# Mirrored rows of x from a reversed copy in DRAM, in a Fourier mixing layer with a gated feed-forward layer

## The chip, the cores and the metric

The kernel runs on one core of one Trainium2 chip. The metric is device time in microseconds; the time before is a median of 654.22 us over three runs (650.11 to 654.27). The engines are named as in the profile: PE does matmuls, PEld loads their weights, DVE, ACT and POOL are the vector, scalar and GpSimd engines, and SP issues most of the DMAs.

## The reference

```python
# x: (8, 3008, 256)
X = np.fft.fft(x, axis=1)
X = np.fft.fft(X, axis=2)
t = X.real.astype(np.float32).reshape(24064, 256)
gate = np.maximum(t @ w_gate, 0.0)          # w_gate, w_val: 256 x 1536
val = t @ w_val
out = (gate * val @ w_out).astype(np.float32)  # w_out: 1536 x 256
```

## The kernel before, in words

Only the real part of the two transforms is wanted, so each batch of 3008 rows is first *folded*: rows are added to and subtracted from their mirror images along the sequence and along the channels. What is left is a set of small cosine and sine matmuls (`family`, `dft_steps`), whose results `U` and `V` feed the feed-forward layer. The transform over the channels is multiplied into the weights beforehand (`WA`, `WB`, `WM`). Channel 128 goes a way of its own: `channel_128` writes it to `FN`, a set of "Nyquist" matmuls at L445 reads `FN`, and its row goes through DRAM (`ch128`) and comes back, spread over all partitions, as `CB` (L780) and as one row of `V` (L783).

**Folding.** A batch comes into `XD` by plain DMAs in natural order (`load_rows`, L94 and L98: six DMAs of about 256 KB and two of one row each) and into `XG` in mirrored order (`load_mirror`, L102: six indirect DMAs that POOL issues, each with a list of row numbers). Two rows of x lie side by side in a "pair" of 512 numbers; the half `r` of a batch has 752 pairs, of which 376 are wanted in reverse. `fold_steps(b)` is a list of (cost, step): six `fold_a` (L113), a small one, `channel_128` (L147, L148), then `load_rows(b + 1)`, six `fold_pq` (L121), `small` (L159, L161), and last `fold_f` and `fold_g` (L128, L137) twice each, with the six gathers of batch b + 1 between them. All of this is POOL's work, except that batch 0 is folded on DVE and POOL.

**When fold steps run.** A batch from 1 on has 36 slots (`slot`), three blocks of twelve, each slot for one tile of 128 hidden channels by 504 (or 497) columns in two mirrored halves. In a slot, PE runs five matmuls of 504 columns and eight output matmuls (L498) of the block before; ACT seeds a bank (L686) and copies (L694); DVE combines (L702) and multiplies (L599); POOL adds (`both`, L703). `run_fold` then adds a credit and takes steps from the list while the credit pays for them; at the end of a batch `run_fold(99)` takes all that are left. The credit is 1.1 x 0.9 in batch 1 and 0.9 x 0.9 in later ones. In batch b, `fold_steps(b + 2)` runs. Batch 0 is done in four segments instead; there POOL folds batches 1 and 2 without slots, up to the last six entries of batch 2, which go over into batch 1.

**Outputs.** A finished output tile is copied by ACT into `os` (L504), which has four buffers, and goes out by two or three DMAs on SP (L513, L516). SP works through its DMAs in program order: outputs, `load_rows`, `ch128`, `CB`, `V`. The build gives each DMA one of eight completion counters in turn, so an issue also waits for the DMA eight issues earlier.

The places that set this order:

```python
    for k in range(6):
        steps += gathers[k:k + 1] + last[k:k + 1]
...
    run_fold(fold_us * (1.6 if not new else .9))
    run_one(evict)
```

Of the kernel before, what the change touches and what calls it, by code (L numbers as in the profile page):

```python
# [10 lines left out]
F32 = mybir.dt.float32  # L11
# [21 lines left out]
def kernel(  # L33
# [8 lines left out]
    nc = tc.nc  # L42
# [57 lines left out]
    def load_mirror(b, t, r):  # L100
# [3 lines left out]
            in_offset=bass.IndirectOffsetOnAxis(ap=gidx[0:n, 2 * t + r:2 * t + r + 1] if t < 2 else gidx2[0:n, r:r + 1], axis=0),  # L104
            element_offset=b * S * D)

    def flat(ap):
        return ap.rearrange("p t q d -> p (t q) d")

# [29 lines left out]
    def fold_steps(b):  # L139

        e, p, ts = nc.gpsimd, slice(0, 128), slice(0, 3)
        steps = [(1.1, lambda r=r, t=t: fold_a(e, p, r, t)) for t in range(3) for r in range(2)]
        steps += [(0.2, lambda: e.tensor_tensor(XG[:, :, :, ::-1, 0], XG[:, :, :, ::-1, 0], XD[:, :, :, :, 0], op=ALU.add))]

        def channel_128():
            for i in range(2):
                e.tensor_tensor(c128p[:, i], XG[:, 0, :, ::-1, 128], XG[:, 1, :, ::-1, 128], op=SIGN[i])  # L147
            e.tensor_tensor(FN[:, :, :, :, b // 2, :, b % 2].rearrange("p i t q h -> p i (t q) h"),  # L148
                            c128p[:].rearrange("p i t q -> p i (t q)").unsqueeze(3).to_broadcast([128, 2, 6, 2]), sg[:], op=ALU.mult)
        steps.append((0.5, channel_128))  # L150
        gathers = []
        if b + 1 < B:
            steps.append((0.0, lambda: load_rows(b + 1)))
            gathers = [(1.3, lambda r=r, t=t: load_mirror(b + 1, t, r)) for t in range(3) for r in range(2)]
        steps += [(1.1, lambda i=i, t=t: fold_pq(e, p, i, t)) for t in range(3) for i in range(2)]

        def small():
            for i in range(2):
                e.tensor_tensor(PQ[:, i, :, :, 0], XG[:, 0, :, ::-1, 0], XG[:, 1, :, ::-1, 0], op=SIGN[i])  # L159
            zero = PQ[:, :, :, :, 0:1].rearrange("p i t q d -> p (i t q) d")  # L160
            e.tensor_tensor(FF[b % 2][:, :, :, :, 0:1].rearrange("p i t q d -> p (i t q) d"), zero, zero, op=ALU.add)  # L161
        steps.append((0.6, small))
        last = []
        for fam in (1, 0):
            last.append((1.7, lambda fam=fam: fold_f(e, p, ts, fam, b)))
            last.append((1.7, lambda fam=fam: fold_g(e, p, ts, fam, b)))
        for k in range(6):
            steps += gathers[k:k + 1] + last[k:k + 1]
        return steps

    load_rows(0, nc.scalar)

# [175 lines left out]
    for n, c in enumerate(order):  # L348
        even_rest(n, c)
        load_mirror(1, n // 2, n % 2)  # L350

# [351 lines left out]
    def slot(cur, mid, nxt, after, outs, fold_us):  # L705

        stop = len(todo_out)

        def out(part):
            run(todo_out, len(todo_out) - stop + outs * part // 8)  # L710
        old = nxt is not None and nxt["kind"] == "o"
        new = nxt is not None and not old
        if old:
            gate(nxt)
        if new and mid["kind"] != "o":
            sine_part(nxt)
        out(3)
        out(5)
        if new and mid["kind"] == "o":
            sine_part(nxt)  # L720
        if new:
            cosine_part(nxt)
        seed(after)
        if pending is not None:
            mirror(pending["v"], pending, 1)
        if pending is not None:
            second(pending)
        value(cur)
        if cur["kind"] == "o":
            mult(cur, 0, cur["first"])  # L730
        else:
            relu_mult(cur, 0)
        if new:
            both(nxt)
        if old:
            nxt["first"] = nxt["r"]
            mirror(nxt["g"], nxt, 0)
            relu(nxt)
        run_fold(fold_us * (1.6 if not new else .9))
        run_one(evict)  # L740
        run_one(sums)
        out(8)
        return cur
# [4 lines left out]
    for b in range(B):  # L748
        blocks = thirds if b else segments
        more_b = {} if b else more  # L750
        if 0 < b < B - 2:
            todo_fold += fold_steps(b + 2)
        for blk, block in enumerate(blocks):
            hs = []
            if (b, blk) == (0, 1):
                todo_dft = dft_steps(0, U, V, (0,), nyq=True, now=True)
            if b == 0 and blk > 1:
                todo_fold = fold_steps(blk - 1)
                later = todo_fold[-6:] if blk == 3 else []
                del todo_fold[len(todo_fold) - len(later):]  # L760
                run_fold(99)
                todo_fold = later
            if blk == (0 if b else 2) and b + 1 < B:
                Un, Vn = new_uv()
                todo_dft = dft_steps(b + 1, Un, Vn, (1, 0), now=not b)
                CBn = up.tile([128, 4 * NJ + 2], BF16, name="CB", tag="CB")
                uv[b + 1] = Un, Vn, CBn
                steps, todo_dft = todo_dft, []
                if b == 0 or b % 2:
                    g, N = (b + 1) // 2, rp.tile([36, NE], BF16, name="N", tag="N", bufs=1)  # L770
                    todo_dft = nyquist_steps(g, N)

                    def keep(N=N, g=g):
                        flush()
                        keep_nyquist(g, N)
                    first = 0 if b == 0 else 18
                    steps[first] = lambda step=steps[first], keep=keep: (keep(), step())

                def row_128(b=b, CBn=CBn):
                    nc.sync.dma_start(out=CBn[:, 0:4 * NJ + 1], in_=dram(ch128, (b + 1) * (4 * NJ + 1), [[0, 128], [1, 4 * NJ + 1]]))  # L780

                def row_0(b=b, Vn=Vn):
                    nc.sync.dma_start(out=Vn[0:1, 0:4 * NJ + 1], in_=ch128[b + 1:b + 2, :])  # L783
                for at, f in ((6 if b == 0 else 21, row_128), (21, row_0)):
                    steps[at] = lambda step=steps[at], f=f: (f(), step())
                todo_dft = todo_dft + steps if b == 0 else steps[:18] + todo_dft + steps[18:]
            per_tile = len(todo_out) // NF
            paired = b > 0
            if (b, blk) == (0, 0):
                for fi in range(NF):  # L790
                    st = tile_of(block, fi, (U, V, CB))
                    add_h(st, hs)
                    pending = first_tile(st, more.get((0, fi), ()))
                mirror(pending["g"], pending, 0)
                relu(pending)
            elif not paired:
                for fi in range(NF):
                    st = tile_of(block, fi, (U, V, CB))
                    add_h(st, hs)
                    tag = {(3, 8): "g", (3, 9): "d", (3, 10): "g", (3, 11): "d"}.get((blk, fi), "p")  # L800
                    last = []
                    if (blk, fi) == (3, 11):
                        last = [lambda: (sine_part(ahead[1]), cosine_part(ahead[1]), both(ahead[1]), seed(ahead[2]))]
                    if (blk, fi) == (3, 9):
                        ahead = [next(tiles) for _ in range(3)]
                        more[(3, 9)] = [lambda: seed(ahead[0], prime())]
                        more[(3, 10)] = [lambda: seed(ahead[1], prime())]
                        more[(3, 11)] = [lambda: (sine_part(ahead[0]), cosine_part(ahead[0]), both(ahead[0]))]
                    pending = single_tile(st, per_tile // 2, more_b.get((blk, fi), ()), last, tag)
                    run(todo_dft, DFT_0[blk - 1][fi])  # L810
            else:
                for fi in range(NF):
                    at = NF * blk + fi
                    cur = ahead.pop(0)
                    add_h(cur, hs)
                    ahead.append(next(tiles, None))
                    pending = slot(cur, *ahead, per_tile, 1.1 if b == 1 else .9)
                    run(todo_dft, DFT_ODD[at] if b % 2 else DFT_EVEN[at])
            run(todo_out, len(todo_out))
            if blk == len(blocks) - 1 or (b, blk) == (0, 1):  # L820
                run(todo_dft, len(todo_dft))
            todo_out = out_steps(b, block, hs)
        if b:
            run_fold(99)
        if b + 1 < B:
            U, V, CB = Un, Vn, CBn
# [31 lines left out]
```

## Time and profile before

| | |
|---|---|
| median of three runs | 654.22 us |
| profiled execution: its time, its span | 654.64 us, 652.4 us |
| mean granted clock of PE | 0.992 |
| busy PE, DVE, POOL, ACT | 95%, 85%, 83%, 70% of the span |
| DMA, mean | 85 GB/s |
| the chain that ended last | PE 67%, DVE 13%, POOL 9% |
| `both` (L703) | 252 x 1251 ns |
| `fold_a` (L113), `fold_pq` (L121) | 42 x 1260 ns, 42 x 1089 ns |
| gathers (L102) | 48 x 1016 ns, 3.7 us to landing |

Busy shares are means over stages with different limits: the first 30 us are tables and weights, batch 0 lasts to about 112 us, and then come seven batches of some 65 to 75 us. The chain's shares tell which engine's work stood last before what followed it, not what would be won if that work were shorter. The granted clock is the share of its full rate that PE's clock was let run at.

### The profile page before, as it was taken

What the parts mean: (1) busy time and instruction counts of PE and PEld (TensorE: products, weight loads), DVE (VectorE), ACT (ScalarE), POOL (GpSimd) and SP (SyncE); (2) the same over time, 40 slices, a digit from 0 to 9 for tenths busy, and PEclk for the clock granted to TensorE, in tenths of its full rate; (3) what the DMA queues carried; (4) which work ended last, traced back from release to release, by engine and by line L of the source; (5) the groups of instructions that cost most, each with busy time, mean ns of one, the idle gap of its engine ahead of it and who ended that gap; (6) DMA issues with size and microseconds to landing.
All of it is one profiled execution on the core that took longest, in us unless ns stands there. A gap on an engine that the chain in (4) does not pass through costs nothing.

```text
span 652.4 us, 12167 instructions
## 1 busy us (share of the span) xinstructions
PE 621.8 (95%) x4140; PEld 401.4 (62%) x4142; DVE 553.1 (85%) x988; ACT 455.3 (70%) x822; POOL 542.0 (83%) x516
## 2 busy tenths in 40 slices
PE   0999999997998999999999999999999999999996
PEld 0356676564665666666666666666666666666665
DVE  8875566995996889989899889989899989999991
ACT  8697666774775777777777777777777777777751
POOL 8589995898999999999899999999986666666660
PEclk9999999997998999999999999999999999999999
DMA  8922653223222422214222332221211121111112
GB/s 224 205 66 63 193 147 99 63 65 128 83 71 78 141 74 80 76 52 143 89 82 79 104 96 92 68 65 40 65 49 33 47 70 52 33 48 49 49 47 80
DMA packets 42438, 55.24 MB, mean 85 GB/s; under 512 B 5153, under 2 KB 32353, under 8 KB 42376
## 3 DMA queue, kind: packets, MB, share of 16 engines
q1 hardware_dynamic: 34552, 39.23, 19.7%
q0 software_dynamic: 7536, 14.72, 8.9%
q8 instruction: 32, 0.52, 0.3%
q10 hardware_dynamic: 288, 0.52, 0.2%
q14 instruction: 30, 0.25, 0.1%
HBM read 32.14 MB, written 24.67 MB: 87 GB/s over the span
## 4 chain that ended last, share of the span: by engine, by line
PE 67%; DVE 13%; POOL 9%; issue 7%; ACT 3%; DMA 0%; DVEq 0%; SPq 0%; ACTq 0%; POOLq 0%
PE o L498 27%; PE v L577 7%; DVE h L599 7%; PE v L572 6%; PE v L573 6%; PE g L691 6%; PE p L698 5%; POOL r L703 5%; DVE r L702 5%; PE d L387 3%; POOL XG L102 1%; PE p L577 1%; POOL XG L113 1%; PE p L573 1%; PE p L572 1%
## 5 line engine op out<-in xcount | busy, mean ns | idle before, releaser
L703 POOL TENSOR_TENSOR r<-r 128x504 f32<-128x504 f32 (+1 forms) x252 | 313.2, 1251 | 73.7 <-DVE r L702 72.6
L599 DVE SCALAR_TENSOR_TENSOR h<-r,v 128x504 bf16<-128x504 f32 (+1 forms) x504 | 318.6, 673 | 51.4 <-PE v L577 34.4
L498 PE MATMUL o<-wo,h 128*128 128x256 bf16 x2304 | 347.0, 273 | 0.0
L498 PEld LDWEIGHTS <-h 128*128 128x128 bf16 x2304 | 226.0, 98 | 116.7 <-issue 3.9
L686 ACT ACTIVATE p<-CB,b 128x504 f32<-128x504 bf16 (+1 forms) x252 | 172.4, 684 | 74.1 <-DVE r L702 72.3
L694 ACT COPY r<-g 128x504 f32<-128x504 f32 (+1 forms) x252 | 145.6, 578 | 76.6 <-PE g L691 72.0
L702 DVE SCALAR_TENSOR_TENSOR r<-r,p 128x504 f32<-128x504 f32 (+1 forms) x252 | 168.8, 670 | 0.6 <-ACT r L694 0.6
L577 PE MATMUL v<-V,WM 128*128 128x504 bf16 (+3 forms) x296 | 109.1, 368 | 3.7 <-DVE h L599 3.1
L572 PE MATMUL v<-U,WA 128*128 128x504 bf16 (+3 forms) x296 | 109.1, 369 | 0.1
L573 PE MATMUL v<-V,WB 128*128 128x504 bf16 (+3 forms) x296 | 109.0, 368 | 0.0
L691 PE MATMUL g<-V,WM 128*128 128x504 bf16 (+1 forms) x252 | 95.2, 378 | 0.4 <-ACT r L694 0.3
L698 PE MATMUL p<-U,WA 128*128 128x504 bf16 (+1 forms) x252 | 95.0, 377 | 0.0
L595 DVE TENSOR_TENSOR h<-r,v 128x376 bf16<-128x376 f32 (+1 forms) x88 | 44.7, 543 | 25.6 <-PE v L577 13.6
L504 ACT COPY os<-o 128x512 f32<-128x512 f32 x96 | 55.6, 579 | 14.1 <-PE o L498 7.1
L572 PEld LDWEIGHTS <-WA 128*128 128x128 bf16 x348 | 34.0, 98 | 42.4 <-issue 13.1
L102 POOL DMA_INDIRECT XG<-in_x_dram,gidx x48 | 48.8, 1016 | 8.8 <-issue 6.8
L573 PEld LDWEIGHTS <-WB 128*128 128x128 bf16 x348 | 34.1, 98 | 35.2 <-issue 1.2
L113 POOL TENSOR_TENSOR XG<-XG,XD 128x510 f32<-128x510 f32 x42 | 52.5, 1260 | 0.1
L587 ACT ACTIVATE r<-p 128x376 f32<-128x376 f32 (+1 forms) x80 | 38.3, 490 | 18.6 <-PE p L577 11.4
L121 POOL TENSOR_TENSOR PQ<-XG 128x510 f32<-128x510 f32 x42 | 45.3, 1089 | 0.0
L577 PEld LDWEIGHTS <-WM 128*128 128x128 bf16 x348 | 34.1, 98 | 7.7 <-issue 0.2
L691 PEld LDWEIGHTS <-WM 128*128 128x128 bf16 x252 | 24.8, 98 | 6.8 <-issue 1.3
(130 smaller groups left out, 380.0 us busy)
## 6 DMA issues: line engine op xcount, KB each, us to landing
out_dram<-os SPq DMA_DIRECT2D x118, 128.0 KB
XD<-in_x_dram SPq DMA_DIRECT2D x30, 256.0 KB
out_dram<-os SPq DMA_DIRECT2D x62, 120.0 KB
XD<-in_x_dram SPq DMA_DIRECT2D x16, 240.0 KB
CB<-ch SPq DMA_DIRECT2D x7, 376.2 KB
out_dram<-os SPq DMA_DIRECT2D x10, 127.0 KB
XG<-in_x_dram,gidx POOLq DMA_INDIRECT x48, 3.7
h<-in_moe_w_gate_dram POOLq DMA_DIRECT2D x3, 256.0 KB, 7.0
```

Of the source, the lines that this page charges most:

```text
L113: e.tensor_tensor(XG[p, r, t, ::-1, 1:D], XG[p, r, t, ::-1, 1:D], XD[p, r, t, :, D - 1:0:-1], op=ALU.add)
L498: nc.tensor.matmul(st["p"][:, q, :], lhsT=hs[f][:, sign, h0:h0 + 128], rhs=wo[:, f, :], start=(f == 0), stop=(f == NF - 1))
L572: nc.tensor.matmul(bank[:, 0:st["n"]], lhsT=WA[i][:, st["f"]], rhs=st["us"], start=True, stop=False)
L573: nc.tensor.matmul(bank[:, 0:st["n"]], lhsT=WB[i][:, st["f"]], rhs=st["vs"], start=False, stop=True)
L577: nc.tensor.matmul(bank[:, 0:st["n"]], lhsT=WM[i][:, st["f"]], rhs=st["vs"], start=False, stop=True, skip_group_check=True)
L599: nc.vector.scalar_tensor_tensor(half_h(st, sign), in0=st["s"][1 + sign][:, 0:n], scalar=0.0, in1=st["v"][:, 0:n], op0=ALU.max, op1=ALU.mult)
L686: nc.scalar.activation(st["p"][:, 0:st["n"]], st["c"], ACTF.Copy, scale=b2[:, st["fi"]:st["fi"] + 1])
L691: nc.tensor.matmul(st["g"][:, 0:n], lhsT=WM[0][:, st["f"]], rhs=st["vs"], start=True, stop=True)
L694: nc.scalar.copy(q[:, 0:n], st["g"][:, 0:n])
L698: nc.tensor.matmul(st["p"][:, 0:n], lhsT=WA[0][:, st["f"]], rhs=st["us"], start=False, stop=True, skip_group_check=True)
L702: nc.vector.scalar_tensor_tensor(sp[:, 0:n], in0=q[:, 0:n], scalar=-0.5, in1=st["p"][:, 0:n], op0=ALU.mult, op1=ALU.add)
L703: nc.gpsimd.tensor_tensor(sm[:, 0:n], sp[:, 0:n], q[:, 0:n], op=ALU.add)
```

## The change

For batches 2 to 7, `XG` no longer comes by gathers. `reverse(b)`, one DMA on SP's queue, copies the wanted rows of batch b to a DRAM tensor `xr` in reverse order: its source runs over 2 halves, 376 pairs at a step backward, and 512 numbers; its destination is contiguous. `load_reversed(b)` then brings them to `XG` by six plain DMAs, and one pair of each half by two DMAs of one row. In the list of fold steps, `load_reversed(b + 1)` stands at no cost between the first and the second pair of `fold_f` and `fold_g`, and `reverse(b + 2)` at no cost at the end. `reverse(2)` is issued at the start. Batches 0 and 1 keep the gathers. The credit becomes 1.05 in batch 1 and 0.7 later, without the factor, and four entries of batch 2's list go over into batch 1.

```diff
+    xr = nc.dram_tensor("xr", (B, 2, H // 4, 2 * D), F32).ap()
+
+    def reverse(b):
+
+        n = H // 4
+        nc.sync.dma_start(out=xr[b], in_=dram(x, b * S * D + (H // 2 - 1) * 2 * D, [[H * D, 2], [-2 * D, n], [1, 2 * D]]))
+
+    def load_reversed(b):
+        n = H // 4
+        for t in range(3):
+            m = (128, 128, 120)[t]
+            for r in range(2):
+                nc.sync.dma_start(out=XG[0:m, r, t, :, :].rearrange("p a d -> p (a d)"), in_=xr[b, 1 - r, 128 * t:128 * t + m, :])
+        for r in range(2):
+            nc.sync.dma_start(out=XG[120:121, r, 2, :, :].rearrange("p a d -> p (a d)"),
+                              in_=dram(x, b * S * D + r * H * D, [[0, 1], [1, 2 * D]]))
...
-        gathers = []
         if b + 1 < B:
             steps.append((0.0, lambda: load_rows(b + 1)))
-            gathers = [(1.3, lambda r=r, t=t: load_mirror(b + 1, t, r)) for t in range(3) for r in range(2)]
...
-        for k in range(6):
-            steps += gathers[k:k + 1] + last[k:k + 1]
-        return steps
+        if b + 1 < B:
+            last.insert(2, (0.0, lambda: load_reversed(b + 1)))
+        if b + 2 < B:
+            last.append((0.0, lambda: reverse(b + 2)))
+        return steps + last
...
         load_mirror(1, n // 2, n % 2)
+    reverse(2)
...
-        run_fold(fold_us * (1.6 if not new else .9))
+        run_fold(fold_us)
...
-                later = todo_fold[-6:] if blk == 3 else []
+                later = todo_fold[-4:] if blk == 3 else []
...
-                    pending = slot(cur, *ahead, per_tile, 1.1 if b == 1 else .9)
+                    pending = slot(cur, *ahead, per_tile, 1.05 if b == 1 else .7)
```

## The prediction

> **What bounds the kernel now.** I read, in this order: the page's busy shares, the windows by batch, the waits, the timelines of PE, POOL and ACT around the two places where PE idles, and last the DMA view.
>
> ```profile
> PE 621.8 (95%) x4140; PEld 401.4 (62%) x4142; DVE 553.1 (85%) x988; ACT 455.3 (70%) x822; POOL 542.0 (83%) x516
> ...
> L102 POOL DMA_INDIRECT XG<-in_x_dram,gidx x48 | 48.8, 1016 | 8.8 <-issue 6.8
> ```
>
> ```profile
> 154.00:161.00 7.00, 6.13 (x27) 2.73 (x28) 1.44 (x3) 2.02 (x4) 5.22 (x8) 0.51 0.88 293
> 205.00:209.00 4.00, 4.00 (x17) 2.17 (x16) 2.96 (x7) 2.47 (x4) 4.00 (x4) 0.57 0.21 64
> ...
> 206.80:281.90 75.10, 75.10 (x498) 48.83 (x497) 67.98 (x117) 53.55 (x93) 73.09 (x67) 0.99 0.29 88
> 281.90:356.90 75.00, 74.94 (x506) 48.47 (x504) 67.75 (x117) 54.13 (x95) 72.04 (x67) 1.00 0.29 89
> 356.90:430.50 73.60, 73.60 (x494) 48.10 (x492) 67.76 (x117) 53.17 (x93) 71.67 (x66) 1.00 0.30 90
> 430.50:505.30 74.80, 74.80 (x506) 48.45 (x504) 67.81 (x117) 54.25 (x95) 64.94 (x59) 1.00 0.16 48
> 505.30:576.00 70.70, 70.70 (x475) 46.25 (x473) 65.83 (x113) 51.20 (x89) 43.79 (x35) 1.00 0.16 50
> ```
>
> The columns after the span are PE, PEld, DVE, ACT, POOL, granted clock, DMA share, GB/s. From batch 2 on PE never idles, and a matmul costs the same with gathers (73.6 us / 494 = 149 ns), without them (74.8 / 506 = 148) and without any fold (70.7 / 475 = 149). POOL's load is therefore hidden there. It shows at two places in batch 1:
>
> ```profile
> PE d L445 <- POOL FN L148: 3.3, 1, 3.3
> PE v L577 <- DVE h L599: 3.1, 4, 2.1
> ...
> 199.57 1.04 POOL L102 DMA_INDIRECT XG<-in_x_dram,gidx  x1 [0.19 <-issue]
> 200.92 1.03 POOL L102 DMA_INDIRECT XG<-in_x_dram,gidx  x1 [0.31 <-issue]
> 203.27 1.27 DVE L599 SCALAR_TENSOR_TENSOR h<-r,v 128x504 bf16<-128x504 f32 x2 [3.00 <-POOL r L703]
> 204.59 0.37 PE L577 MATMUL v<-V,WM 128*128 128x504 bf16 x1 [2.14 <-DVE h L599]
> ```
>
> At 151.6 the Nyquist matmuls wait 3.3 us for `channel_128`, and the clock then stands at half (0.51 over 7 us: 3.4 us lost). At 202.5 two gathers stand ahead of a `both`; PE loses 2.1 us and then 1.7 us to the clock (0.57 over 4 us).
>
> **What is removed.** 36 gathers leave POOL, 36 x 1.016 = 37 us plus some 7 us of issue gaps. The worth is what PE gets: 3.3 + 3.4 + 2.1 + 1.7 = 10.5 us. Batch 1 to its `channel_128` held four gathers (119.7 to 135.8) at about 1.2 us; without them, and at a credit of 1.05 a slot where 1.1 x 0.9 = 0.99 stood, `FN` is ready some 10 us before PE asks, so I take the whole gain. Batches 2 to 4: between 0 and 1 us each (their 148 to 151 ns a matmul against 148 without gathers); I take 1.5 in all. The credits: a `both` (1.25) and 1.05 of fold make 2.3 us of POOL a slot against PE's two; lag costs nothing until `both` is some 3 us late (the 3.00 wait above). Batch 1 may pass that: 0 to 3.5 us, taken as 1. At 0.7 the sum is 1.95 and hidden. Net: **-11 us** (bounds -13.5 and -7).
>
> **What is added on SP.** Per batch, eight loads into `XG` and one copy. The loads are like XD's, some 0.45 us an issue; six XD loads land within 7 us, one slot of 36 needs them, and POOL reads them ten or more slots later. Only in batch 0, where POOL goes straight from fold 1 to fold 2, can POOL wait for them, by some 5 us, before it has a `both` to deliver at 112.7: zero. SP has idle time for 9 issues (it waits 406 us for `os`). They wait for POOL's `small`; the outputs behind them need ACT's `os` later than that: zero too.
>
> The copy `reverse` is another matter. It moves 752 rows of 2 KB, and its source has 2 as its outermost count. How wide does a DMA run? The trace has two of small shape. The output of 127 rows issued at 273.1 ran alone like this (columns: 40 slices of 277.7 to 279.4 us):
>
> ```profile
> GB/s 410 24 313 217 506 24 313 410 313 120 169 506 121 169 24 410 24 72 120 72 24 24 24 24 24 24 24 24 24 24 24 24 24 24 24 24 24 24 24 24
> ```
>
> The peaks are a gather; the floor of 24 GB/s is that output, one row after another, 1 KB in 42 ns: a single engine. `ch<-N` at 317, with 2 outermost on one side and 4 on the other, posts one early completion event and then two: two engines. So I count two engines for `reverse`: 1.54 MB / (2 x 24 GB/s) = **32 us**. Bounds: 30 (25.6 GB/s an engine, a 410 slice above over 16) and 40 (376 rows x 106 ns, the mean of XD's 2 KB packets, which share engines). DRAM to DRAM stands nowhere in the trace; I stay at the low end because nothing else is queued ahead.
>
> And what stands behind it? The 128-row output issued right after that 127-row one got 15 of its 16 completions by 277.2 us and the last at 282.8, when the 127 rows were through. So a DMA on SP's queue waits, on each engine that it shares, for what was issued before. Everything that SP issues within 32 us of a `reverse` lands after it: 1.3 us to start (XD: issue 152.99, first packet 154.3), 32 of copy, 0.7 to land: **34 us** from its issue.
>
> The Trainium skill, page DMA: Bandwidth & Descriptors, section Rules for kernel authors, says that an outermost dimension below 16 confines a DMA to that many engines; here that is 2, as counted. The same page's table in section Bandwidth gives 341 GB/s for 1 MB, by which the copy would take about 4.5 us (an estimate from that table) and the sum would be 642 rather than 682; its rows are for 128 partitions, and the 24 GB/s row above speaks for the first.
>
> **Where that stalls.** `os` has four buffers, so a copy L504 waits until the outputs four tiles back have landed. ACT's copies in steady state:
>
> ```profile
> 254.84 0.58 ACT L504 COPY os<-o 128x512 f32<-128x512 f32 x1
> 260.61 0.58 ACT L504 COPY os<-o 128x512 f32<-128x512 f32 x1
> 266.39 0.58 ACT L504 COPY os<-o 128x512 f32<-128x512 f32 x1
> 272.17 0.58 ACT L504 COPY os<-o 128x512 f32<-128x512 f32 x1
> 280.89 0.58 ACT L504 COPY os<-o 128x512 f32<-128x512 f32 x1
> 284.94 0.58 ACT L504 COPY os<-o 128x512 f32<-128x512 f32 x1
> ```
>
> Behind a stuck L504 ACT holds the next slot's L694 and L686; PE runs on for about one slot, 1.8 us, which I subtract each time.
>
> - `reverse(2)`, about 31 to 65 us: `os` is written first at 49.3, the fifth time at 80. Zero.
> - `reverse(3)`, issued at about 75.5 (after XD's and XG's loads), landed 109.5. In the built program SP waits at the eighth DMA behind it for the copy itself; ten issues later (4.6 us) follows CB's load, behind XD's 1.5 MB (7.7 us from issue to last packet when batch 3's came at 91.6). CB lands at about 118.5; the first L686 wants it at 107.7. 10.8 - 1.8 = 9.
> - `reverse(4)`, about 117.5, landed 151.5; the output behind it has 127 rows on one engine, 5.4 us more: 157. L504 at 151.7 wants that buffer, and the next one is 1 us worse: 6.3 - 1.8 = 4.5.
> - `reverse(5)`, right behind CB's issue at 167.7, landed 201.7, wanted by the copy at 194.6: 7.1 - 1.8 = 5.3.
> - `reverse(6)`, `reverse(7)`: behind the outputs of the copy like 254.84, so issued at 256.2, landed 290.2, wanted at 284.94: 5.3 - 1.8 = 3.5 each.
>
> Together 9 + 4.5 + 5.3 + 3.5 + 3.5 = **25.8 us**. PE idle of 2.1 and 3.3 us was followed by 1.7 and 3.4 us lost to the clock: 2.5 for each of five, **12.7**.
>
> **Sum.** The profiled execution took 654.64 (span 652.4), 0.4 above the median of 654.22: 654.6 - 11 + 25.8 + 12.7 = **682 us**. With 30 us of copy, 1.7 of clock each and 1.2 us more slack, the five stalls shrink by 2.5 each: 654.6 - 13 + 13.3 + 8.5 = 663. With 40 us and 3.4: 654.6 - 9 + 25.8 + 41 + 17 = 729.
>
> **Rivals.**
> 1. The copy does not hold the queue: it spreads over 16 engines or yields to what is behind. For it: 1.5 MB of XD landed in 7 us. Against: the 127-row output and the late sixteenth completion. Then only POOL's relief is left: 654.6 - 11 to - 13.5 = 641 to 643.6, faster. It decides once the copy takes under some 20 us, as then no buffer and no CB is late.
> 2. The stalls of `os` are absorbed (copy of about 27 us, or more slack than a slot), and only CB in batch 0 is late: 654.6 - 11 + 9 + 3.4 = 656, no change. Against: the low bound of the copy is 30.
> 3. DRAM to DRAM rows cost 106 ns or more: 715 to 729. For it: XD's mean under load; against: two engines alone have no neighbour.
> 4. POOL at 2.3 us a slot becomes batch 1's bound: 3.5 instead of 1. It shifts the sum by 2.5 only, to 684.5, and is inside the forecast's range.
>
> **How the numbers follow.** Forecast (with 4) 0.62, its own range 663 to 715; rival 3 0.14; rival 2 0.09; rival 1 0.15. One per cent, 6.5 us, is about what a measurement of this kernel can tell from no change. Faster by more: rival 1, 0.15. Within: rival 2 less its edges, 0.08. Slower: 0.77. The range is 646 to 718: it leaves out most of rival 1 and the upper end of rival 3, under 2 in 10.
>
> **What would show it.** Right: six bursts of about 48 GB/s for 32 us; CB's landing and the first L686 late by about 10 us; L504 waiting for DMA `out_dram<-os` some 5 us, four times; granted clock 0.5 right behind; no wait of L445 for FN. Wrong: copies of 5 us at 300 GB/s, or L504 with no DMA wait, with a span near 640.

## The result, and the profile after

The changed kernel takes a median of 696.3 us (692.97 to 697.5, four runs) beside 652.17 us of the kernel before on the same chip (650.11 to 654.27, four runs): a ratio of 1.067, interval 1.061 to 1.073. It is slower by 44 us. The forecast was 682, in a range of 646 to 718. The profiled execution took 696.21 us, with a span of 694.4 and a mean granted clock of 0.970; the spans differ by 694.4 - 652.4 = 42.0 us. Undisturbed runs of before lie between 650.0 us, with a granted clock of 1.0, and 655.1 us, with 0.992; its profiled execution (654.64 us, 0.992) is one of the longer ones, and only these have lost clock to win back. Line numbers move by 18 in the changed kernel: the copy into `os` is L522, its stores L531 and L534, ACT's seed L704, `CB` L798; `reverse` is L112 and the loads from `xr` L119.

The busy shares of the page, after:

```profile
PE 630.4 (91%) x4142; PEld 403.9 (58%) x4142; DVE 554.2 (80%) x988; ACT 454.2 (65%) x822; POOL 506.7 (73%) x480
```

POOL lost its 36 gathers (542.0 to 506.7 us), as planned, and the end did not come earlier. The windows by batch, after (a window from the first combine of DVE in batches 1 to 5 to that of the next; columns after the span: PE, PEld, DVE, ACT, POOL, granted clock, DMA share, GB/s):

```profile
125.80:206.20 80.40, 75.29 (x479) 46.53 (x478) 66.81 (x114) 53.76 (x95) 69.47 (x61) 0.97 0.35 112
206.20:298.80 92.60, 76.11 (x495) 48.99 (x493) 68.12 (x118) 53.12 (x93) 66.18 (x60) 0.91 0.29 94
298.80:379.50 80.70, 76.70 (x506) 48.92 (x505) 67.85 (x117) 53.77 (x95) 66.16 (x60) 0.98 0.32 102
379.50:459.90 80.40, 76.40 (x495) 49.06 (x493) 68.05 (x118) 53.00 (x93) 66.28 (x60) 0.96 0.32 102
459.90:534.60 74.70, 74.70 (x505) 48.36 (x504) 67.71 (x117) 54.09 (x95) 66.08 (x60) 1.00 0.16 48
```

Batches 2 to 4 took 77.6, 75.0 and 73.6 us before. Now PE idles in each of the first four, and its busy time grows as well, since the clock drops. From batch 5 on, when no copy is issued any more, the old length is back. The stalls themselves, in the timeline of ACT (idle time before the instruction and what ended it in brackets):

```profile
111.40 0.58 ACT L522 COPY os<-o 128x512 f32<-128x512 f32 x1 [6.62 <-DMA out_dram<-os]
121.05 0.69 ACT L704 ACTIVATE p<-CB,b 128x504 f32<-128x504 bf16 x1 [6.35 <-DMA CB<-ch]
172.84 0.58 ACT L522 COPY os<-o 128x512 f32<-128x512 f32 x1 [5.83 <-DMA out_dram<-os]
227.36 0.58 ACT L522 COPY os<-o 128x512 f32<-128x512 f32 x1 [17.80 <-DMA out_dram<-os]
319.96 0.59 ACT L522 COPY os<-o 128x512 f32<-128x512 f32 x1 [5.12 <-DMA out_dram<-os]
400.79 0.58 ACT L522 COPY os<-o 128x512 f32<-128x512 f32 x1 [5.17 <-DMA out_dram<-os]
```

One stall for each copy from `reverse(3)` on, and two for that one. What they make of PE, in the waits:

```profile
PE g L709 <- ACT r L712: 28.4, 4, 16.5
PE g L595 <- ACT r L605: 10.8, 3, 6.5
```

No row names the Nyquist matmuls waiting for `FN` any more. The copies themselves, in the DMA view of 195 to 217 us, while `reverse(5)` runs (40 slices):

```profile
GB/s 59 17 45 67 52 45 52 52 52 52 52 52 52 45 52 52 52 52 52 52 52 45 52 52 52 52 82 52 52 45 52 52 52 52 52 52 52 45 52 52
```

52 GB/s, flat: two engines at 26 GB/s each. The copy's 752 packets of 2 KB lie between 195.2 and 226.2 us: 31 us for 1.54 MB, where the prediction had 48 GB/s and 32 us. And SP's own timeline shows something that the prediction did not have:

```profile
137.74 20.96 SPq L531 DMA_DIRECT2D out_dram<-os  x1
158.74 8.42 SPq L534 DMA_DIRECT2D out_dram<-os  x1
...
168.69 6.95 SPq L94 DMA_DIRECT2D XD<-in_x_dram  x6
...
192.68 0.65 SPq L112 DMA_DIRECT2D xr<-in_x_dram  x1
193.44 24.70 SPq L531 DMA_DIRECT2D out_dram<-os  x1
```

The first store behind a copy, from `reverse(3)` on, holds SP in its issue for 19 to 25 us; before, no issue on SP took over 2.9. The sign was there to read: the three issues of before over 2 us, at 195.5, 273.1 and 421.7 us (2.2, 2.6 and 2.9), each stand right behind a store of 127 rows. One of these stores, issued at 272.8 us, is the one that the prediction read as running on a single engine (it says 273.1). So SP itself is late after a copy, and with it all that stands later in its order.

### The profile page after: what moved, and what is told of

Its sections match the earlier page's. It is cut to its first block, busy times and chain, and to the rows that moved or that the text cites. A ratio compares the mean times of both kernels' runs of the same rounds, so it can differ in the third digit from the quotient of the medians.

```text
span 694.4 us, 12187 instructions
## 1 busy us (share of the span) xinstructions
PE 630.4 (91%) x4142; PEld 403.9 (58%) x4142; DVE 554.2 (80%) x988; ACT 454.2 (65%) x822; POOL 506.7 (73%) x480
## 4 chain that ended last, share of the span: by engine, by line
PE 57%; DVE 16%; DMA 12%; issue 7%; SPq 4%; ACT 4%; POOL 1%; DVEq 0%; ACTq 0%; POOLq 0%
PE o L516 22%; DVE h L617 9%; DVE r L720 6%; PE v L595 6%; PE g L709 5%; PE v L590 5%; PE v L591 5%; PE p L716 5%; DMA out_dram<-os 5%; DMA xr<-in_x_dram 5%; PE d L405 3%; SPq L531 2%; SPq L534 1%; DMA XD<-in_x_dram 1%; DMA CB<-ch 1%
## 5 line engine op out<-in xcount | busy, mean ns | idle before, releaser
L704 ACT ACTIVATE p<-CB,b 128x504 f32<-128x504 bf16 (+1 forms) x252 | 172.6, 685 | 78.0 <-DVE r L720 70.9
L720 DVE SCALAR_TENSOR_TENSOR r<-r,p 128x504 f32<-128x504 f32 (+1 forms) x252 | 169.0, 671 | 27.4 <-ACT r L712 27.4
L522 ACT COPY os<-o 128x512 f32<-128x512 f32 x96 | 55.6, 579 | 56.4 <-DMA out_dram<-os 44.8
L590 PEld LDWEIGHTS <-WA 128*128 128x128 bf16 x348 | 34.2, 98 | 41.7 <-issue 12.7
L145 POOL TENSOR_TENSOR F<-PQ 128x768 bf16<-128x768 f32 (+2 forms) x16 | 27.3, 1708 | 0.0
```

The costliest lines, as they stand in the source:

```text
L522: nc.scalar.copy(os_[:], st["p"][:])
L590: nc.tensor.matmul(bank[:, 0:st["n"]], lhsT=WA[i][:, st["f"]], rhs=st["us"], start=True, stop=False)
L704: nc.scalar.activation(st["p"][:, 0:st["n"]], st["c"], ACTF.Copy, scale=b2[:, st["fi"]:st["fi"] + 1])
L720: nc.vector.scalar_tensor_tensor(sp[:, 0:n], in0=q[:, 0:n], scalar=-0.5, in1=st["p"][:, 0:n], op0=ALU.mult, op1=ALU.add)
```

## The experiments

Stage lengths are read in each kernel's trace from DVE's combines: a batch begins with every 36th. The first column is the time at which batch 1 begins, the next are lengths in us; batch 6 lasts 73.6 us everywhere. The runs of before that were taken beside these kernels have medians of 652.09 to 653.16 us; each ratio is to the runs taken beside that kernel. Batches 1 and 2 of before, with 79.5 and 77.6 us, are longer than the 65 to 75 us said ahead.

| kernel | median us | ratio to before (interval) | batch 1 begins | 1 | 2 | 3 | 4 | 5 |
|---|---|---|---|---|---|---|---|---|
| before | 652.17 | 1 | 111.9 | 79.5 | 77.6 | 75.0 | 73.6 | 74.8 |
| changed | 696.3 | 1.067 (1.061 to 1.073) | 125.8 | 80.5 | 92.5 | 80.8 | 80.3 | 74.8 |
| one early copy | 646.38 | 0.992 (0.990 to 0.995) | 111.7 | 75.8 | 73.6 | 75.0 | 73.6 | 74.8 |
| seven `os` | 660.89 | 1.015 (1.011 to 1.018) | 125.7 | 75.7 | 74.3 | 75.0 | 73.6 | 74.8 |
| pieces | 686.65 | 1.054 (1.051 to 1.058) | 126.1 | 100.3 | 73.9 | 75.0 | 73.6 | 74.8 |
| ACT's queue | 681.46 | 1.047 (1.043 to 1.050) | 130.4 | 91.8 | 73.6 | 75.0 | 73.6 | 74.8 |
| sixteen engines | 646.05 | 0.989 (0.987 to 0.991) | 112.3 | 75.8 | 73.6 | 75.0 | 73.6 | 74.8 |
| 2, 3, 4 joined | 670.96 | 1.027 (1.024 to 1.029) | 112.3 | 75.7 | 86.5 | 81.0 | 80.8 | 74.8 |
| copies alone | 705.01 | 1.078 (1.075 to 1.081) | 125.1 | 87.1 | 85.5 | 86.6 | 84.2 | 74.8 |
| GpSimd's queue | 672.42 | 1.031 (1.028 to 1.035) | 132.0 | 81.0 | 74.6 | 75.5 | 73.5 | 74.8 |
| credits alone | 654.84 | 1.004 (1.002 to 1.006) | 112.0 | 77.5 | 74.6 | 76.7 | 75.2 | 76.5 |
| one early copy, old credits | 645.8 | 0.989 (0.986 to 0.991) | 111.7 | 75.0 | 73.6 | 75.0 | 73.6 | 74.8 |
| the same, seven `os` | 645.58 | 0.990 (0.988 to 0.993) | 111.6 | 75.0 | 73.6 | 75.0 | 73.6 | 74.8 |

**One early copy.** All six batches go as one DMA where `reverse(2)` stood; nothing else is copied later.

```diff
-        nc.sync.dma_start(out=xr[b], in_=dram(x, ..., [[H * D, 2], [-2 * D, n], [1, 2 * D]]))
+        nc.sync.dma_start(out=xr[b:B].rearrange("b h n d -> (b h) n d"),
+                          in_=dram(x, ..., [[H * D, 2 * (B - b)], [-2 * D, n], [1, 2 * D]]))
...
-        if b + 2 < B:
-            last.append((0.0, lambda: reverse(b + 2)))
...
```

The list of fold steps is one entry shorter by this, and three entries of batch 2's list go over into batch 1 in place of four, so the same steps go over. In the other kernels whose list changes by a copy's entry the number is set the same way.

> One copy for batches 2 to 7 where reverse(2) stood (12 halves outermost, so 12 engines), and the five later copies left out; all else as in the changed kernel. Theory: a copy keeps two engines for 31 us and SP, which issues everything else, stands still meanwhile; this is the whole loss. Then the one copy runs from 31 to some 62 us, where no output needs its buffer: no L522 waits for a DMA, CB is on time, and the time is that of before less the 10.5 us that batch 1 lost to POOL: 640 to 644. Rival: the loads into XG, the bytes or the credits carry part of the loss: 655 or more, with the copies out of the way.

Measured 646.38 us, 2 above the expected interval, and 0.8% under the kernel before. All the loss is gone, so the later copies made it, not the loads from `xr` or the credits. Its stages against those of before also give the gain by itself: 3.7 us in batch 1, 4.0 in batch 2, nothing later, 652.4 - 644.6 = 7.8 us of span. Between the medians (652.09 for the runs of before beside it) it is 5.7, because the profiled execution of before, at 654.64 us, lies above that median.

**Seven buffers of `os`.**

```diff
-                os_ = rp.tile([128, 2, D], F32, name="os", tag="os", bufs=4)
+                os_ = rp.tile([128, 2, D], F32, name="os", tag="os", bufs=7)
```

> Seven os buffers where four stood; all else as in the changed kernel. SP is held as before, but ACT has 18 us more before it needs a buffer. Theory (the os buffers carry the loss of reverse(4) to reverse(7), CB's landing that of reverse(3)): waits of L522 under 5 us in all, the first L704 still waits for CB, some 13 us now that no L522 waits ahead of it: 655 to 663. Rival (late XD, XG or CB loads carry the loss in later batches as well): 675 or more.

Measured 660.89 us, inside. Its waits:

```profile
ACT p L704 <- DMA CB<-ch: 13.0, 1, 13.0
...
ACT os L522 <- DMA out_dram<-os: 1.4, 1, 1.4
```

The copies still hold SP's queue (SP stands 25.2 us in the store behind `reverse(5)`), but ACT does not want a buffer before they are through. From batch 1 on the stages are those of one early copy, but for 0.7 us in batch 2. Only `CB`, which no buffer helps, is late, and that is nearly all of the 14.4 us of span left: batch 1 begins at 125.7 us, 14.0 late.

**Sixteen engines.** The same six DMAs, places and bytes, with 16 outermost. This kernel leaves out the mirrored order of the rows, so its results for batches 2 to 7 are not the reference's; it is there for its time alone.

```diff
-        nc.sync.dma_start(out=xr[b], in_=dram(x, ..., [[H * D, 2], [-2 * D, n], [1, 2 * D]]))
+        nc.sync.dma_start(out=xr[b].rearrange("h n d -> (h n) d").rearrange("(a j) d -> a j d", a=16),
+                          in_=dram(x, b * S * D, [[2 * D, 16], [32 * D, n // 8], [1, 2 * D]]))
```

> The six copies of the changed kernel at their places, each with the same 752 rows of 2 KB in SP's queue, but laid out with 16 as the outermost count instead of 2; the rows are taken in another order than the mirrored one, so the values of batches 2 to 7 are not the reference's. Theory (what costs is that a copy sits on two of the sixteen engines for 30.5 us, with SP and the stores of os behind it): at 26 GB/s an engine 1.54 MB are 4 us, with 47 rows on each engine, and the kernel is the one with a single early copy, 645 to 650 us, with no wait for os over 1 us that the kernel with one early copy (2.0 us) does not have, and CB not late. Rival (the bytes, or six more DMAs in SP's row ahead of the outputs, cost, whatever their width): 675 us or more.

Measured 646.05 us, with the waits of one early copy: `os` 2.0 us once, and no row for `CB`.

```profile
ACT os L523 <- DMA out_dram<-os: 2.0, 1, 2.0
```

So neither the bytes nor the place in SP's order cost anything: the width does. The source is also stepped through forward here, but that is not the reason: the one early copy steps backward on twelve engines, and its DMA view has a mean of 307 GB/s between 60 and 61.2 us, 26 GB/s an engine as on two. SP's timeline at `reverse(5)`:

```profile
166.99 0.62 SPq L112 DMA_DIRECT2D xr<-in_x_dram  x1
167.71 13.44 SPq L532 DMA_DIRECT2D out_dram<-os  x6
```

The second row covers six stores and SP's waits for ACT between them; the first store was issued in 0.57 us, not 24.7. The Trainium skill, page DMA: Bandwidth & Descriptors, section Rules for kernel authors, has the rule on which the prediction leaned, that an outermost count under 16 confines a DMA to that many engines at most; the 52 GB/s above and this run agree.

**The copies alone.** The kernel before, gathers and credits included, with the six copies at their places. Nothing reads `xr`.

> The kernel before with its gathers and its credits, and the six copies of the changed kernel added at the changed kernel's places; nothing reads what they write. Theory (the copies alone cost what the change costs and gives back; the reads of the mirrored rows add little): 652.1 + 42 + 7.8 = 695 to 705 us, with the waits for os and for CB of the changed kernel. Rival (the loss needs the new loads of XG in SP's row behind each copy): 655 to 675 us.

Measured 705.01 us, at the upper edge. The copies make the loss with or without the new loads, and the gathers' leaving takes some of it back. The timeline of ACT in this kernel has the same stalls at other lengths, since the order on SP is another; two of them:

```profile
251.76 0.58 ACT L514 COPY os<-o 128x512 f32<-128x512 f32 x1 [6.96 <-DMA out_dram<-os]
336.92 0.59 ACT L514 COPY os<-o 128x512 f32<-128x512 f32 x1 [10.54 <-DMA out_dram<-os]
```

**Copies 2, 3 and 4 joined.** One DMA, outermost count 6, at the place of `reverse(2)`; `reverse(5)` to `reverse(7)` stay.

```diff
+        c = 3 if b == 2 else 1
-        nc.sync.dma_start(out=xr[b], in_=dram(x, ..., [[H * D, 2], [-2 * D, n], [1, 2 * D]]))
+        nc.sync.dma_start(out=xr[b:b + c].rearrange("b h n d -> (b h) n d"),
+                          in_=dram(x, ..., [[H * D, 2 * c], [-2 * D, n], [1, 2 * D]]))
...
-        if b + 2 < B:
+        if 5 <= b + 2 < B:
...
```

> The copies for batches 2, 3 and 4 go as one DMA (outermost count 6) where the copy for batch 2 stands; those for batches 5, 6 and 7 stay. Four buffers of os. Theory (the copy for batch 5 cost 14.9 us in the changed kernel because SP was late from the copy for batch 4 and issued it after the first store of the block, not ahead of it): now it is issued in time and costs what the copies for batches 6 and 7 cost there (5.8 and 6.7); three of them on the kernel with one early copy: 646.4 + 6 to 8 + 5.8 + 6.7 = 665 to 668 us. Rival (the copy for batch 5 has a costly place of its own): 646.4 + 18.7 + 5.8 + 6.7 = 675 to 679 us.

Measured 670.96 us: between the two. The timelines of SP and of ACT, and the window of batch 2, in this kernel:

```profile
167.31 0.65 SPq L113 DMA_DIRECT2D xr<-in_x_dram  x1
...
202.47 0.58 ACT L523 COPY os<-o 128x512 f32<-128x512 f32 x1 [11.15 <-DMA out_dram<-os]
```

```profile
188.00:274.50 86.50, 76.66 (x495) 49.06 (x493) 68.01 (x117) 53.00 (x93) 66.06 (x60) 0.92 0.31 96
```

`reverse(6)` and `reverse(7)` cost 81.0 - 75.0 = 6.0 and 80.8 - 73.6 = 7.2 us, as expected. `reverse(5)` costs 86.5 - 73.6 = 12.9: 6 less than the 18.9 in the changed kernel, and 5 more than the forecast's 7.8. Both parts were real: SP's lateness, and a place worse than reckoned.

**In pieces.** The copies for batches 5 to 7 are cut into eight DMAs of two times 47 rows, between fold steps; 2 to 4 stay whole.

```diff
+    def reverse_piece(b, k):
+        m = H // 32
+        nc.sync.dma_start(out=xr[b, :, m * k:m * k + m, :],
+                          in_=dram(x, b * S * D + (H // 2 - 1 - m * k) * 2 * D, [[H * D, 2], [-2 * D, m], [1, 2 * D]]))
...
-        if b + 2 < B:
+        if b + 2 < B and b < 3:
...
```

> The copies of batches 5, 6 and 7 cut into eight DMAs of 94 rows each, still on two engines and on SP's queue, spread over the fold steps of the batch; batches 2 to 4 as in the changed kernel. Theory (SP stands still because it can hand over only so many rows ahead): each piece is 47 rows an engine, 4 us, and SP goes on at once; the waits of L522 behind reverse(5) to reverse(7), 17.8, 5.1 and 5.2 us with the clock behind them, shrink to what reverse(4) leaves: 662 to 670. Rival (the same bytes on the same two engines delay whatever follows): 685 or more.

Measured 686.65 us: a miss, the number of the rival for another reason. Where only pieces are left, batches 2 to 4, the stages are 73.9, 75.0 and 73.6: the pieces are as good as free on the same two engines. The loss is in what lies before: batch 1 begins 14.4 us late, as in the changed kernel, and lasts 100.3 us, where that took 80.5. The timeline of SP shows why:

```profile
132.75 0.66 SPq L112 DMA_DIRECT2D xr<-in_x_dram  x1
133.46 25.04 SPq L116 DMA_DIRECT2D xr<-in_x_dram  x1
```

The first piece for batch 5 now stands right behind the whole copy for batch 4, holds SP for 25.0 us, and lies ahead of all stores; `os` then comes late by 9.2 and 9.8 us, `CB` by 6.5. I had put a DMA at a place where SP's queue was already full.

**ACT's queue.** The copies are issued from ACT in place of SP.

```diff
-        nc.sync.dma_start(out=xr[b], ...)
+        nc.scalar.dma_start(out=xr[b], ...)
```

> The six copies issued by ACT instead of SP, still on two engines; all else as in the changed kernel. Theory: SP's issue is held by its own queue alone. From ACT's queue the copy shares the two engines row by row with the outputs, SP's longest issue is under 3 us, L522 does not wait, ACT pays about 0.7 us an issue: 640 to 648. Rival: whatever hands rows to the engines is shared by both queues, or ACT itself is held: 685 or more.

Measured 681.46 us: a miss for the theory. Batches 2 to 4 are free of loss (73.6, 75.0, 73.6), with the copies for 5 to 7 as narrow as ever. The loss is before batch 1 (18.7 us against one early copy) and in it (16.0). What SP waited for:

```profile
SPq L94 <- DMA xr<-in_x_dram: 46.3, 2, 31.9
SPq L534 <- DMA xr<-in_x_dram: 37.2, 2, 18.6
```

No store is held in its issue behind `reverse(3)` (0.34 to 0.51 us each), but at the eighth DMA after it SP stands 31.9 us until the copy has landed: the build gives the DMAs of both queues the same completion counters in turn. This was a wait of the program, not of the queue. The shared engines are felt, though: behind `reverse(4)`, `reverse(6)` and `reverse(7)` the store right after one of 127 rows, which runs on a single engine, held SP for 8.3, 7.3 and 7.3 us, where such stores took 1.2 to 2.9 us in the kernel before. How the 16.0 us in batch 1 divide between these holds and SP's waits is not shown.

**GpSimd's queue.** The same edit with `nc.gpsimd`, whose DMAs count on other counters.

> The six copies at their places, still two engines wide, but issued from GpSimd's queue. With ACT's queue SP was no longer held in the issue behind a copy, but it stood at the eighth DMA after each copy, waiting for that copy (46.3 us at two loads of XD, 37.2 and 27.8 us at outputs), since DMAs of SP and ACT take turns on the same completion semaphores in the built program. Theory (SP's standing still is the loss, the two shared engines cost little): GpSimd's DMAs count on others, so SP does not stand, and the kernel is the one with one early copy plus six issues on GpSimd: 646 to 654 us. Rival (each load and output has a part on the two busy engines and comes late there, whichever queue the copy is in): 665 to 685 us, with CB and os late again.

Measured 672.42 us: the rival's number, and `os` and `CB` are late again in batch 0 (10.9 and 7.6 us). By stages it is again both: from batch 2 on 74.6, 75.5 and 73.5, within 1 us of no loss, but batch 1 begins at 132.0 and lasts 81.0. The DMA issues and the waits of SP in this kernel:

```profile
xr<-in_x_dram POOLq DMA_DIRECT2D x6, 1504.0 KB, 39.5
```

```profile
SPq L119 <- DMA xr<-in_x_dram: 19.9, 1, 19.9
```

GpSimd came to issue `reverse(2)` only at 54.4 us, where SP had issued it at 31. A copy takes 39.5 us from issue to landing there, so SP stood 19.9 us at the first load of `XG` that reads it, with batch 0's stores, `XD` and `CB` behind it. This order accounts, as far as the waits tell, for the larger part of the 20.3 us by which batch 1 begins later than with one early copy, but sharing the two engines has a part in it: behind that wait SP stood another 10.5 us, between 95 and 115 us, for loads of `XG` that ran beside `reverse(3)`, where one early copy has 4.0 us of such waits in all. In batch 1, 5.2 us longer than with one early copy, two loads of `XD` beside `reverse(4)` held SP for 4.2 us each and `os` came 3.7 us late; what each cost is not shown. In batches 2 to 4 the sharing was worth at most 1.0 us a batch. The Trainium skill, the same page, section Queues, rings and completion order, says that a DMA engine takes turns between the queues that have work for it, and drains each queue's ring in order. The stages from batch 2 on in these two runs agree: with the narrow copy in SP's own queue batches 2 to 4 take 80.3 to 92.5 us, with it in another queue 73.5 to 75.5.

**The credits.** Alone, on the kernel before; and the old ones on the kernel with one early copy:

```diff
-        run_fold(fold_us * (1.6 if not new else .9))
+        run_fold(fold_us)
...
-                    pending = slot(cur, *ahead, per_tile, 1.1 if b == 1 else .9)
+                    pending = slot(cur, *ahead, per_tile, 1.05 if b == 1 else .7)
```

> The kernel before with its gathers, and only the new credits for fold steps. Theory (with one early copy the old credits were 0.8 us faster in batch 1 and the same elsewhere; with the gathers still on GpSimd the new credits move fold steps into other slots and cost no more than that): 652 to 655 us. Rival (a higher credit in batch 1 brings channel_128 forward and takes the Nyquist wait away): 646 to 650 us.

> The kernel with one early copy, with the credits of the kernel before. Theory (the gain of 5.7 us comes from the gathers leaving GpSimd, the credits are worth about 1 us): 645 to 648 us. Rival (the new credits carry the gain): 650 to 653 us.

Measured 654.84 us and 645.8 us, both where the theory had them. With the gathers still there, the new credits take 2.0 and 3.0 us off batches 1 and 2 and put 1.7, 1.6 and 1.7 on the next three. Without gathers the old credits are 0.8 us faster in batch 1 and the same elsewhere. The credits are worth under 1 us in the change.

**One early copy, old credits, seven `os`.**

> One early copy, the credits of the kernel before, seven buffers of os. Theory (after the early copy has landed only one wait for os of 2.0 us is left, hidden by PE's slack): 645 to 646.5 us, no difference from the four buffers (645.8). Rival (that wait reaches PE): 642.5 to 644 us.

Measured 645.58 us, no difference from 645.8. The last wait for `os` was hidden. These two are the fastest kernels of the study, about 1% under the kernel before (both intervals end below 1).

## Why the prediction was right or wrong

Against one early copy, which has all of the change but the repeated narrow copies, the changed kernel's span is 694.4 - 644.6 = 49.8 us longer. PE's busy time, with the same matmuls, is 630.4 - 617.8 = 12.6 longer (the clock); the other 37.2 are idle time (64.0 against 26.8). So the sum reads, in spans:

| term | predicted | measured |
|---|---|---|
| relief of POOL | -11 | -7.8 |
| stalls | 25.8 | 37.2 |
| clock | 12.7 | 12.6 |
| sum | 27.4 | 42.0 |

*Width and rate of the copy, and the order behind it*: right. 26 GB/s on each of two engines, and the store's buffer came free 34.7 us after the issue of `reverse(5)` (192.68 to 227.36), for 34 predicted. Sixteen engines, everything else kept, give the time of one early copy.

*Clock*: right, 12.6 for 12.7, and not only in the sum: from batch 0 to 4 PE's busy time is 3.8 (two stalls), 1.9, 2.4, 1.8 and 2.7 us longer than with one early copy, for 2.5 a stall. The records can mislead, though: they show half clock for 17 us around `reverse(5)` (216 to 233 us), most of it while PE idled, and the busy time of that batch grew by only 2.4 us.

*Relief of POOL*: the wait for `channel_128` is gone, and so is the late `both`. The second, in batch 2 by the table of stages, was worth 4.0 (3.8 predicted). The first was worth 4.5 with the old credits, where 3.3 of idle time and 3.4 of clock were predicted: in that kernel PE idles 2.2 us less in batch 1 and is busy 2.2 us less. The credit cost 0.8 (1 predicted), and the 1.5 for batches 2 to 4 were not there: with sixteen engines, or one early copy, batches 3 and 4 last 75.0 and 73.6 us, as before.

*Stalls, one by one*, PE's idle time before the first matmul behind each, beside the prediction (they sum to 39.0, 1.8 more than the difference in idle time above):

| copy | predicted | PE idle |
|---|---|---|
| `reverse(3)` | 9 | 6.48 + 4.08 = 10.6 |
| `reverse(4)` | 4.5 | 3.98 |
| `reverse(5)` | 5.3 | 16.49 |
| `reverse(6)` | 3.5 | 3.95 |
| `reverse(7)` | 3.5 | 4.00 |

At `reverse(3)` the sum is nearly right and its parts are not: the prediction had only `CB` late; `os` was, too, 6.62 us just ahead of it. Seven buffers show that the two are one stall: without the wait for `os`, `CB` is 13.0 us late, PE idles 12.2 us in one piece, and batch 1 begins as late. That 9 came so near 10.6 is thus partly luck.

**The step that was mis-sized is `reverse(5)`: 5.3 us predicted, 16.5 measured**, which is 11.2 of the 13.2 us by which the five together (39.0) exceed their prediction. The prediction had the copy of `os` 26.9 us behind the issue (167.7 to 194.6), a wait of 7.1. Two things were missing, and the joined kernel tells them apart:

- *The gain took away the stall's slack.* The 194.6 was read in the trace of before, in which PE had waited for `FN` in that batch and then run at half clock. The change takes that away, so the copy comes at 191.3 (in the kernel with sixteen engines, whose batch 1 begins within 0.4 us of that of before), 3.3 us earlier, while `CB`, and `reverse(5)` behind it, are issued at 167, as they were. In the joined kernel the issue is at 167.31 and the wait ends at 202.47, 0.8 later than the 201.7 predicted: 7.1 + 3.3 + 0.8 = 11.2, and 11.15 were measured.
- *SP was late from the copy before.* The prediction let SP go on at some 0.45 us an issue up to the eighth DMA behind a copy. In the changed kernel the stores behind `reverse(4)` held SP for 21.0 and 8.4 us; eight loads of `XD`, eight of `XG` and `CB` followed late, and `reverse(5)` was issued at 192.68. The copy of `os` that waits would have been at 227.36 - 17.80 = 209.56, 16.9 us behind that issue in place of 24.0 (167.31 to 191.32) in the joined kernel. So the wait grows to 17.8. The prediction put each copy at its place in the timeline of before, and let no copy push the next.

The copy of `os` of the first point, in the timelines of before and of sixteen engines:

```profile
194.63 0.58 ACT L504 COPY os<-o 128x512 f32<-128x512 f32 x1
...
191.29 0.58 ACT L523 COPY os<-o 128x512 f32<-128x512 f32 x1
```

*Rivals.* The first, a copy that does not hold the queue, is what the kernel with sixteen engines is; its price of 641 to 643.6 was 2 to 5 us too low, by the terms of the relief. The second, `os` absorbed and only `CB` late (656), is nearly what seven buffers make of it: 660.89. The third, rows at 106 ns, fell with the 52 GB/s. The fourth, POOL as batch 1's bound, was 0.8 us.

*Not settled:* how much of the loss behind `reverse(4)` is SP held in its issue and how much is the order of rows on the two engines, since in SP's queue both come together; how the losses of batches 0 and 1 in the other two queues divide between SP's waits and the shared engines; and what the first copies would cost in another queue if they were issued early and counted by themselves.

## What to carry to other kernels

Here a DMA's outermost count decided how many engines it ran on (52 GB/s with 2, 307 with 12), and what stood behind a narrow DMA in its queue waited for it: cost such a DMA by the rows on one engine, and count what stands behind it. When several such holds follow each other, carry the lateness of each into the issue time of the next, and read the times at which their results are wanted only after the gains of the change are taken off. Where the work of several narrow DMAs can be issued as one, early, while nothing urgent waits behind it, it can be free: here that turns 44 us of loss into 6 us of gain.

## What the runs showed of the hardware

The issuing sequencer is held, too. Behind a copy with 376 rows for each of two engines, SP's next issue took 19 to 25 us. Behind `reverse(5)` it ended at 218.1 us, 8 us before the copy's last row at 226.2, when some 200 packets of 2 KB, 100 for each engine, were still to go. Behind the other copies of that kernel from `reverse(3)` on the same count is 96 to 107 an engine. The early copy, at 26 GB/s on each of twelve engines, held SP as well: 11.6 us in the store at 49.7. Copies with 47 rows for an engine held it not at all with sixteen engines (0.57 us). In the kernel with pieces the issues behind a piece that stood alone took 0.25 to 0.4 us; where two to four pieces followed each other in batch 1 (171 to 199 us), single issues took 2.2 to 8.3 us, while two later pairs, 2.6 and 2.2 us apart (at 258 and 333 us), held nothing. This points to a limit on what is queued on an engine, and not to the time that the DMA takes; its exact size was not measured.
